# Linear attention's normaliser moved from the numerators to phi(Q), and the output weight folded into KV

## The chip, the cores and the metric

The kernel runs on one core of a Trainium2 chip. The metric is device time in microseconds for one execution. The engines named below are TensorE (PE, with its weight loads shown apart as PEld), VectorE (DVE), ScalarE (ACT), GpSimd (POOL) and SyncE (SP, which issues DMAs here).

## The reference, cut to what matters

Two attention branches read the same input x (2048 tokens, 512 features, 32 heads of 16) and are mixed by a gate per token:

```python
g = sigmoid((x * gate_w).sum(-1, keepdims=True))
# A: softmax attention
p = softmax(einsum("bhqd,bhkd->bhqk", q, k) * Dh**-0.5)
a = einsum("bhqk,bhkd->bhqd", p, v) -> (S, D) @ A_wo
# B: linear attention, own q, k, v from B_wqkv
phi = lambda t: where(t > 0, t + 1, exp(t)) + 1e-6
kv  = einsum("bhsd,bhse->bhde", phi(k), v)
z   = phi(k).sum over s
num = einsum("bhqd,bhde->bhqe", phi(q), kv)
den = einsum("bhqd,bhd->bhq", phi(q), z) + 1e-6
b   = (num / den) -> (S, D) @ B_wo
out = g * a + (1 - g) * b
```

Branch B can be regrouped: num @ B_wo equals, head by head, phi(q) @ (kv @ B_wo), and a division by den that is the same for all 16 columns of a head may be applied to phi(q) before either product.

## The kernel before, in words

**Scores.** A round is one query chunk of 512 tokens for four heads; there are 32 rounds. A round has 64 units, each a 128x512 tile of scores (one key block of 128, one head), 2048 units in all. A loop over groups (from L2160) takes two or three units at a time: TensorE computes their scores into PSUM banks 0 to 5, and one ScalarE instruction (L2239) takes the exp of all of them into the ring PT. Beside them VectorE "claims" further units: `claim` (near L1746) has TensorE write one more score tile into a spare bank or an unused third bank of a group, and VectorE turns it into an approximate exponential by writing integers that are read as float16 (DP). Four claimed units make a buffer; two shifted copies of it are made by an integer add, which GpSimd does nearly always (L1790) and VectorE otherwise (L1787). TensorE multiplies each PT tile by V once and each claimed tile by V three times (the copy and its two shifts, with weights), into an accumulator bank; at a round's end VectorE evicts it (L1475), and the softmax denominators travel by small DMAs on SyncE to a reciprocal and back, broadcast to `rbc`, for a product on VectorE (L1463).

**Everything else** (projections, branch B, the output) is a list of steps. A step runs TensorE pieces into the one spare bank (bank 7 and the accumulator's bank change places from time to time) and ends with VectorE or ScalarE work that empties it. While the bank is held by a step it can't carry a claimed unit. The steps have due times, spread over the groups: branch B's run from the 6th to about the 310th.

**Who sets the order.** The program is written out straight by a planner in Python that keeps a clock for every engine with estimated durations. It fills the time between two groups: products with V, a due step, a claim, in an order set by thresholds (class K, `OPTIONS`). The list `ORDER` picks a value for each threshold anew for every window of eight groups, so each row changes what follows. VectorE's waiting work is a pool of items (`push`), picked by priority and estimated start. A claim is taken only if the estimated VectorE backlog is below a threshold, a bank is free and a DP buffer is free. GpSimd and VectorE work without PSUM operands are kept from overlapping as far as the planner's estimates go: a GpSimd instruction waits for the last such VectorE instruction.

**Branch B before.** `step_BK` (16 steps): phi(K), by `phi_post`: an exp on ScalarE (L1136) and two VectorE instructions (L1139, L1141). `step_gate` and `step_Z`: rows of sums that VectorE copies to SBUF (L1126, L1196) and four small DMAs turn into columns (L1095). `step_M` (4): x times phi(K), evicted at L1175. `step_KV`: KV for all heads, masked to its diagonal blocks (L1215). `step_BQ` (16): phi(Q) of a chunk of 512 queries. `step_den` (4): 1/den times (1-g)/g for 512 tokens x 32 heads (L1242 to L1245). `step_num` (16, one per 128 tokens): phi(Q) times KV, evicted with a product by 1/den on VectorE (L1267) into `OB`, and a DMA transpose (L733) into `OBT`, the operand of the output matmuls. `step_out` (its first eviction starts at 518.7 us) accumulates branch B's and branch A's output in one bank and scales it by g on eviction (L1332).

Of the kernel before, what the change touches and what calls it, by code (L numbers as in the profile page):

```python
# [22 lines left out]
class K:  # L23
# [28 lines left out]
    ('EVEN', (2, 0, 5, 8)),  # L52
)
ORDER = [
    "000000000000000000000000",
    "000000000000000000000000",
    "000000000000000000000000",
    "000000000000000000000000",
    "000000000000000000000000",
    "000000000001000000000000",  # L60
    "000000200201000000000000",
    "000000000000000000000000",
    "000000000000000000000000",
    "000000200000000000100000",
    "000000000000000000000002",
    "000000000000000000000000",
    "000000000000000000000000",
    "000000000000000000002001",
    "010000001000000000000000",
    "000000200000000000000000",  # L70
    "000000000000000000000000",
    "000000000000000000000000",
    "000000000000000000000000",
    "000001000200000000000000",
    "000001000200020000000000",
    "000000200000000000000000",
    "000000000001000000000000",
    "000000030000000000000000",
    "000000030001000000000000",
    "000000000002000000000000",  # L80
    "100000200002000000000000",
    "000000000000000000000000",
    "000100200000000000100000",
    "000100200100000001100000",
    "000000030000000000000000",
    "000020030002001000000000",
    "000020000000000000000000",
    "000020000100000000000000",
    "000000000000000000000000",
    "000010000000001000000003",  # L90
    "200010000000001000000003",
    "000000000000000000000000",
    "000000000000000000000000",
    "000000100000000000000000",
    "000002020000000000000000",
    "000000000000000010000000",
    "000000000000020000000000",
    "000020000000020000020000",
    "000000000000000000000000",
    "000000000001000001000000",  # L100
    "000000000000000000000002",
    "000000000000000000000000",
    "000000000000000000000000",
    "000000002000200001000000",
    "010000202000200011002000",
    "000000000000020000001000",
    "000000000100200000000000",
    "200020000000000000100000",
    "200020200000100000200000",
    "200020200100100000001000",  # L110
    "000000010100000000000000",
    "000000000000000000000000",
    "000000000000000010000010",
    "000000000002000010000010",
    "000000000000000000000000",
    "000000000000000000000000",
    "000000000000000010000000",
    "000000100000000000000000",
    "010000100000000000200000",
    "000000000000000000020010",  # L120
    "000000000110000000000000",
    "200000000100010000000000",
    "000000200000010000000000",
    "000000002000000000000000",
    "000000012000000000000000",
    "000000000000000000000001",
    "010001000000000000000000",
    "000000000000000100000000",
    "000000000100000000000000",
    "300000000200000000000000",  # L130
    "000000000000000000000000",
    "000020200000010000000000",
    "200020200000010000200000",
    "000000000002000000000000",
    "000000000001010000000000",
# [27 lines left out]
E_MAX = 1.0e26  # L163
# [102 lines left out]
class _Res:  # L266

    __slots__ = ("name", "w", "r", "tw", "tr", "we", "pend", "pw")

    def __init__(self, name):  # L270
        self.name = name
        self.w = None
        self.r = {}
        self.tw = 0.0
        self.tr = 0.0
        self.we = None
        self.pend = 0
        self.pw = 0

# [58 lines left out]
def bass_gated_mix__mha_block__linear_attn_block__prompt_kernel(  # L338
# [33 lines left out]
    with ExitStack() as es:  # L372
# [66 lines left out]
        Zsel = SB([128, NCC, 8], BF16, "Zsel")  # L439

        phiK = SB([128, 2, 4, D], BF16, "phi")
        phiQT = phiK

        xnat = phiQT[:].rearrange("p a i n -> p (a i n)").rearrange("p (b c) -> p b c", b=NTB)
        rdB = SB([128, 2, 128], FP32, "rdB")

        OB = SB([128, 4, D], BF16, "OB")
        MT = OB
# [4 lines left out]

        def obt(tb):
            if tb < NTB // 2:
                return wB[:, :, D + 128 * tb:D + 128 * (tb + 1)]
            return OBT2[:, :, 128 * (tb - NTB // 2):128 * (tb + 1 - NTB // 2)]
# [6 lines left out]
        wide = OB[:].rearrange("p a n -> p (a n)").bitcast(FP32)[:, 0:512]  # L464
# [29 lines left out]
        semN = [SEM(f"s_n{k}") for k in range(5)]  # L494
        n_counts = [0] * 5
        semOB = [SEM(f"s_ob{b}") for b in range(NTB)]
# [9 lines left out]
        r_wA, r_warm, r_wB, r_woA, r_woB = R("wA"), R("warm"), R("wB"), R("woA"), R("woB")  # L506
# [8 lines left out]
        r_PT = [R(f"PT{i}") for i in range(NPT)]  # L515
        r_DP = [[R(f"DP{i}{k}") for k in range(NTRI)] for i in range(NB)]
# [15 lines left out]
        r_phiQT = r_phiK  # L532
        r_rdB = [R("rdB0"), R("rdB1")]
        r_OB = [R(f"OB{i}") for i in range(4)]
        r_OBT = [R(f"OBT{b}") for b in range(NTB)]
# [5 lines left out]
        r_wide = r_OB[0:2] + r_MT  # L541
# [49 lines left out]
        def blocker(it, reads, writes):  # L591
            for other in sorted((x for x in items if x.seq < it.seq), key=lambda x: x.seq):
                if any(conflicts(o, reads, writes) for o in other.ops):
                    return other
            return None
# [44 lines left out]
        def settle(reads, writes):  # L640

            while True:
# [82 lines left out]

        def flush_items():
            while items:
                it = min(items, key=lambda i: i.seq)
                emit_item_op(it)
# [40 lines left out]
        def dma_batch(pairs, sem, reads, writes, total_after, lands=3.0):  # L770
# [5 lines left out]
            SP.t = st + 0.59 * len(pairs)  # L776
# [78 lines left out]
        for t in range(1, NQC):  # L855
# [5 lines left out]
        op(PO, lambda: nc.gpsimd.memset(gw[:], 0.0), writes=[r_gw], dur=0.1)  # L861
        dma(gw[:, :, 0:1], gate_w.rearrange("(cc p o) -> p cc o", p=128, o=1), semG, writes=[r_gw], total_after=16, noncontig=True, E=SP,
            lands=8)
        xt_all = [r_xT[c][t] for c in range(NCC) for t in range(NQC)]
# [45 lines left out]
        op(PO, lambda: nc.gpsimd.memset(ones32[:, 0:1], 1.0), writes=[r_ones32], dur=0.1)  # L910
        op(PO, lambda: nc.gpsimd.memset(dev[:], OK_MID), writes=[r_dev], dur=0.2)
# [84 lines left out]
        def step_K(t8, t, early=False, on_act=False, lo=0, n=512, **kw):  # L996
# [4 lines left out]
            def post(b):  # L1001
                src = bank_ap(b)[:, 0:n]
                if on_act:
                    op(AC, lambda: nc.scalar.copy(KT[:, par, c0:c1], src), reads=[r_bank[b]],
                       writes=[r_KT[par][t]], dur=0.16 + n * 8.3e-4)
                    return
                push(1, [(lambda: nc.vector.tensor_copy(KT[:, par, c0:c1], src),  # L1007
                          [r_bank[b]], [r_KT[par][t]], d_psum(n), None)])
# [17 lines left out]
        def step_Q(t8, qc, early=False, **kw):  # L1026
# [3 lines left out]
            def post(b):  # L1030
# [8 lines left out]
                push(1, [(lambda: nc.vector.tensor_scalar(Qs[:, src, :], bank_ap(b), CQ, None, op0=ALU.mult),  # L1039
# [6 lines left out]
        def step_V(t8, v, early=False, **kw):  # L1046
# [13 lines left out]
            def post(b):  # L1060
# [14 lines left out]
                push(1, ops)  # L1075
# [13 lines left out]
        def row_to_columns(dst, sem, r_dst):  # L1089

            settle(r_wide, r_dst)
            st = est_start(SP, r_wide, r_dst)
            deps = _deps_for(r_wide, r_dst)
            for j in range(4):
                SP.add(lambda j=j: nc.sync.dma_start(dst(j), wide[32 * j:32 * j + 1, :]), deps, inc=False, dma_sem=sem, dma_val=64)  # L1095
            SP.t = st + 0.59 * 4
            for res in r_wide:
# [7 lines left out]

        def step_gate(**kw):
            rd = xt_all + [r_gw]

            def pieces(b):
                o = bank_ap(b)  # L1110
                fns = [[f_row(o, j, gw[:, cc, :], xT[:, cc, 512 * j:512 * (j + 1)], start=(cc == 0), stop=(cc == NCC - 1))
                        for j in range(4)] for cc in range(NCC)]
                return [(fns[k] + fns[k + 1], rd, 2 * MM512, 2 * MM512, "cols") for k in (0, 2)]

            def post(b):
                def moved():
                    row_to_columns(lambda j: eg[:, 4 * j:4 * j + 4], semRow[0], [r_eg])
                    push(1, [(lambda: nc.vector.tensor_single_scalar(eg[:], eg[:], -1.0, ALU.mult), [r_eg], [r_eg], 0.18, negated)])

                def negated():  # L1120
                    op(AC, lambda: nc.scalar.activation(eg[:], eg[:], ACT.Exp), reads=[r_eg], writes=[r_eg], dur=0.25, issue=0.2)  # L1121
                    push(1, [
                        (lambda: nc.vector.tensor_single_scalar(gom[:, 1, :], eg[:], E_MAX, ALU.min), [r_eg], [r_g], 0.18, None),
                        (lambda: nc.vector.tensor_single_scalar(gom[:, 0, :], gom[:, 1, :], 1.0, ALU.add), [r_g], [r_g], 0.18, None),
                        (lambda: nc.vector.reciprocal(gom[:, 0, :], gom[:, 0, :]), [r_g], [r_g], 0.25, None)])
                push(1, [(lambda: nc.vector.tensor_copy(wide.rearrange("p (q k) -> p q k", k=4), bank_ap(b).rearrange("p (k q) -> p q k", k=4)), [r_bank[b]], r_wide, d_psum(512) + 0.06, moved)])  # L1126
# [1404 lines left out]
```

## Time and profile before

| what | value |
|---|---|
| median of 3 runs | 656.63 us (656.48 to 656.77) |
| span of the profiled execution, first to last instruction | 655.0 us (the page gives no other time of it) |
| ScalarE busy | 641.3 us, 98% |
| TensorE busy / weight loads | 637.0 us, 97% / 188.3 us, 29% |
| VectorE busy | 577.0 us, 88% |
| GpSimd busy | 366.6 us, 56% |
| granted TensorE clock | 1.000 |

A row of a group of instructions reads: line, engine, operation, tile written and tile read, shapes, count, then total busy time, mean time of one in ns, and the idle time of the engine just ahead of them with what ended it. L826 is the line of a helper that records every matmul, so matmuls are told apart by their tiles. A row of a table by stretch gives the stretch, its length, the busy time of PE, PEld, DVE, ACT and POOL with counts, then the granted clock, the DMA engines' share and GB/s; limited to one line of the kernel, only its engine is given.

### The profile page before, as it was taken

How to read it: one execution, taken by the hardware profiler on the slowest of the kernel's cores; microseconds unless marked ns; L12 is line 12 of the kernel's file. 1: busy time of each engine (PE TensorE's matmuls, PEld its weight loads, DVE VectorE, ACT ScalarE, POOL GpSimd, SP SyncE). 2: the span in 40 equal slices, each digit the busy share in tenths (PEclk: the TensorE clock that was granted, in tenths of full speed). 3: DMA queues.
4: the chain of work that ended last, by engine and by line, in shares of the span. 5: the costliest groups of instructions: out<-in, count | busy, mean ns of one | idle time of the engine just before them, and what ended most of it. 6: DMA issues, size and time to landing. Idle time of an engine off the chain costs nothing.

```text
span 655.0 us, 18894 instructions
## 1 busy us (share of the span) xinstructions
PE 637.0 (97%) x7881; PEld 188.3 (29%) x7881; DVE 577.0 (88%) x994; ACT 641.3 (98%) x702; POOL 366.6 (56%) x365
## 2 busy tenths in 40 slices
PE   8999999999999999999999999999999999999997
PEld 4322222332223233233222233232222222222223
DVE  6588999989888887999999999999989989879984
ACT  5999999999999999999999999999999999999995
POOL 6055566555565554544474656566767656646650
PEclk9999999999999999999999999999999999999999
DMA  9900101001022010101202002020101001010111
GB/s 212 272 6 8 29 3 32 6 11 28 3 56 46 15 23 3 35 11 28 41 11 45 16 15 39 17 53 11 27 11 27 19 23 39 18 43 19 43 26 38
DMA packets 45968, 22.97 MB, mean 35 GB/s; under 512 B 35128, under 2 KB 41720, under 8 KB 45880
## 3 DMA queue, kind: packets, MB, share of 16 engines
q1 hardware_dynamic: 43864, 20.14, 13.9%
q10 hardware_dynamic: 2016, 1.57, 0.9%
q8 instruction: 65, 1.06, 0.7%
q14 instruction: 23, 0.19, 0.1%
HBM read 8.00 MB, written 2.10 MB: 15 GB/s over the span
## 4 chain that ended last, share of the span: by engine, by line
ACT 81%; PE 18%; DVE 0%; issue 0%; POOL 0%; ACTq 0%; POOLq 0%
ACT PT L2239 79%; PE ps L826 17%; ACT epool L1136 2%; PE ps L833 0%; DVE DP L2341 0%; DVE Qpad L1035 0%; DVE KT L1007 0%; DVE DP L2346 0%; DVE flag L2351 0%; POOL warm L871 0%; POOL gw L861 0%; POOL dummy L843 0%; ACT eg L1121 0%; ACTq L2454 0%; POOLq L2516 0%
## 5 line engine op out<-in xcount | busy, mean ns | idle before, releaser
L2239 ACT ACTIVATE PT<-ps 128x1024 bf16<-128x1024 f32 (+1 forms) x662 | 632.1, 1211 | 1.2 <-PE ps L826 0.9
L1790 POOL INT64_ADD DP<-DP x345 | 355.3, 1040 | 267.3 <-DVE DP L1746 201.1
L1746 DVE TENSOR_SCALAR DP<-ps 128x512 int16<-128x512 f32 x694 | 451.6, 683 | 42.4 <-PE ps L826 37.1
L826 PE MATMUL ps<-Qpad,KT 32*128 32x512 bf16 x2048 | 261.6, 384 | 11.3 <-ACT PT L2239 5.4
L826 PE MATMUL ps<-DP,Vaug 128*32 128x512 f16 x2077 | 200.2, 384 | 0.0
L826 PE MATMUL ps<-PT,Vaug 128*32 128x512 bf16 x1344 | 156.9, 384 | 1.0 <-DVE oraw L1475 0.5
L826 PEld LDWEIGHTS ps<-Qpad,KT 32*128 32x128 bf16 x2048 | 66.4, 91 | 282.9 <-ACT PT L2239 258.5
L826 PEld LDWEIGHTS ps<-DP,Vaug 128*32 128x32 bf16 x2077 | 47.1, 95 | 61.7 <-issue 42.8
L826 PEld LDWEIGHTS ps<-PT,Vaug 128*32 128x32 bf16 x1344 | 36.6, 94 | 44.2 <-issue 36.1
L826 PE MATMUL ps<-xT,wA 128*32 128x512 bf16 x432 | 33.0, 384 | 0.0
L1136 ACT ACTIVATE epool<-ps 128x512 bf16<-128x512 f32 x32 | 26.2, 817 | 0.0
L1475 DVE COPY oraw<-ps 128x512 f32<-128x512 f32 x31 | 21.1, 680 | 1.0 <-PE ps L826 1.0
L826 PE MATMUL ps<-warm 128*32 128x512 bf16 (+1 forms) x113 | 20.4, 401 | 1.2 <-POOL warm L871 1.2
L826 PE MATMUL ps<-wB,xT 128*32 128x512 bf16 x256 | 19.7, 384 | 0.0
L826 PE MATMUL ps<-xT,wB 128*32 128x512 bf16 x256 | 19.1, 384 | 0.0
L826 PE MATMUL ps<-woA,OT 128*32 128x512 bf16 (+1 forms) x226 | 18.9, 384 | 0.0
L1141 DVE SCALAR_TENSOR_TENSOR phi<-ps,epool 128x512 bf16<-128x512 f32 x24 | 16.5, 686 | 0.5
L1139 DVE TENSOR_SCALAR epool<-epool 128x512 bf16<-128x512 bf16 x32 | 9.3, 292 | 6.7 <-ACT epool L1136 6.3
L1007 DVE CAST KT<-ps 128x512 bf16<-128x512 f32 (+1 forms) x16 | 10.7, 666 | 5.2 <-PE ps L826 5.2
L826 PE MATMUL ps<-wA,xT 128*128 128x128 bf16 x192 | 14.9, 220 | 0.0
L1062 DVE CAST Vaug<-ps 128x512 bf16<-128x512 f32 x16 | 10.9, 682 | 2.3 <-PE ps L826 2.3
L826 PEld LDWEIGHTS ps<-wA,xT 128*128 128x128 bf16 x192 | 10.8, 98 | 5.4 <-issue 4.5
(115 smaller groups left out, 224.0 us busy)
## 6 DMA issues: line engine op xcount, KB each, us to landing
rbc<-oraw SPq DMA_DIRECT2D x16, 256.0 KB
OT<-in_A_x_dram SPq DMA_DIRECT2D x4, 512.0 KB, 7.3
Qpad<-Qs SPq DMA_DIRECT2D x124, 16.0 KB, 1.8
oraw<-oraw SPq DMA_DIRECT2D x60, 32.0 KB, 1.9
wA<-in_A_wqkv_dram SPq DMA_DIRECT2D x1, 1536.0 KB, 7.9
wB<-in_B_wqkv_dram SPq DMA_DIRECT2D x1, 1536.0 KB, 8.9
out_dram<-outt SPq DMA_DIRECT2D x12, 128.0 KB, 1.7
phi<-in_A_x_dram ACTq DMA_DIRECT2D x3, 256.0 KB, 6.0
```

Source lines behind the costliest of these rows:

```text
L826: return lambda: nc.tensor.matmul(o, lhsT=l, rhs=r, start=start, stop=stop, skip_group_check=sg)
L1007: push(1, [(lambda: nc.vector.tensor_copy(KT[:, par, c0:c1], src), [r_bank[b]], [r_KT[par][t]], d_psum(n), None)])
L1062: ops = [(lambda: nc.vector.tensor_copy(v_group(NQC * par + v)[:, :, :, 0:16], src), [r_bank[b]], [r_V[par][v]], d_psum(512), lambda: v_do ...
L1136: op(AC, lambda: nc.scalar.activation(epool[:, s, :], bank_ap(b), ACT.Exp), reads=[r_bank[b]], writes=[r_e[s]], dur=0.6, issue=0.48)
L1139: (lambda: nc.vector.tensor_scalar(epool[:, s, :], epool[:, s, :], 1.0, 1e-6, op0=ALU.min, op1=ALU.add), [r_e[s]], [r_e[s]], 0.29, None),
L1141: (lambda: nc.vector.scalar_tensor_tensor(out=dst, in0=bank_ap(b), scalar=0.0, in1=epool[:, s, :], op0=ALU.max, op1=ALU.add), [r_bank[b], ...
L1475: push(0, [(lambda: nc.vector.tensor_copy(oraw[:, half, :], acc), [r_acc], [r_oraw[half]], d_psum(512), evicted)])
L1746: push((0 if in_group else 1) + K.PRIO_NEW, [(lambda: nc.vector.tensor_scalar(DP[:, i, 512 * k:512 * (k + 1)].bitcast(I16), bank_ap(b), FR ...
L1790: ops = (*ops[:4], None, POOL_ADD, lambda z=z, i2=i2, i=i, n=n: nc.gpsimd.int64_add(DP[:, i2, 0:n].bitcast(I64), DP[:, i, 0:n].bitcast(I64 ...
L2239: op(AC, lambda p0=p0, b0=b0, n=n: nc.scalar.activation(PT[:, 512 * p0:512 * p0 + n], ps[:, 512 * b0:512 * b0 + n], ACT.Exp, scale=LN2 / F ...
```

## The change

- KV times the output weight: the KV step exchanges its operands, so that KVbd holds KV transposed, and four new steps (`step_W`) multiply it by each 128 rows of B_wo and write the result over `woB`. The numerators (`step_num`), their buffer OB and the 16 DMA transposes are gone.
- phi(Q) of each chunk is written straight to the place from which the output matmuls read it (`phiq`), and multiplied there by 1/den: `step_den` computes the denominators with heads along the partitions (Zsel has 32 columns now), VectorE adds, inverts and scales as before in three instructions, four DMAs gather the result into rows, four DMAs spread each head's row over its 16 partitions, and GpSimd makes four products of 128x512 per chunk (16 in all).
- The spreading DMAs are issued late: `later` holds them back until the planner's clock says that the gathered rows have landed.
- The gate step comes after KV. Its exp reads the bank directly on ScalarE, with the sign in its scale; VectorE's wide copy, its sign flip and one small step go. Its columns come in another order (`gcol`).
- The memset of gw becomes a GpSimd copy after its load; Zsel gets a memset.
- Five more thresholds can vary (`NEW_LATE`, `PRIO_EV`, `MARGIN`, `MIN_LAST`, `THIRD`), and `ORDER` is another list. The first option of each new threshold is the old constant, or no effect, except that `PRIO_EV` of 1 is the old priority of evictions and -1 puts them first.
- The planner counts thirds of units in whole numbers instead of fractions, and skips some searches.

```diff
+    ('NEW_LATE', (0, 1)),
+    ('PRIO_EV', (1, -1)),
+    ('MARGIN', (0.19, 0.1, 0.3)),
+    ('MIN_LAST', (20, 12, 28)),
+    ('THIRD', (30, 3)),
 )
 ORDER = [
...
+        later = []
+        def go_later(now=1e9):
+            while later and later[0][0] <= now:
+                later.pop(0)[1]()
...
-        op(PO, lambda: nc.gpsimd.memset(gw[:], 0.0), writes=[r_gw], dur=0.1)
+        push(1, [(lambda: nc.gpsimd.tensor_copy(gw[:, :, 1:32], gw[:, :, 0:1].to_broadcast([128, NCC, 31])), [r_gw], [r_gw], 0.0, None, 0.35)])
...
             def post(b):
-                def moved():
-                    row_to_columns(lambda j: eg[:, 4 * j:4 * j + 4], semRow[0], [r_eg])
-                    push(1, [(lambda: nc.vector.tensor_single_scalar(eg[:], eg[:], -1.0, ALU.mult), [r_eg], [r_eg], 0.18, negated)])
...
+                op(AC, lambda: nc.scalar.activation(gq.rearrange("p t q -> p q t"), bank_ap(b).rearrange("p (q t) -> p q t", q=NQC),
+                                                    ACT.Exp, scale=-1.0), reads=[r_bank[b]], writes=r_gqs, dur=0.6, issue=0.48)
+                row_to_columns(lambda j: eg[:, 4 * j:4 * j + 4], semRow[0], [r_eg], lambda j: gq[32 * j:32 * j + 1, :, :], r_gqs)
+                push(1, [
+                    (lambda: nc.vector.tensor_scalar(gom[:, 1, :], eg[:], E_MAX, 1.0, op0=ALU.min, op1=ALU.add), [r_eg], [r_g], 0.18, None),
+                    (lambda: nc.vector.reciprocal(gom[:, 0, :], gom[:, 1, :]), [r_g], [r_g], 0.25, None)])
...
+        def step_W(i, **kw):
+            rd = [r_KVbd, r_woB[i]]
+            def pieces(b):
+                return [(f_cols(bank_ap(b), KVbd[:, i, :], woB[:, i, :]), rd, MM512, MM512, "cols")]
+            def post(b):
+                push(K.PRIO_EV, [(lambda: nc.vector.tensor_copy(woB[:, i, :], bank_ap(b)), [r_bank[b]], [r_woB[i]], d_psum(512), None)])
+            return Step(pieces, post, reads=rd, **kw)
...
         def step_den(qc, **kw):
...
+                return [([f_mm(o[32 * m:32 * m + 32, 0:128], Zsel[:, i, :], phiq(qc)[:, i, 128 * m:128 * (m + 1)],
+                               start=(i == 0), stop=(i == NCC - 1), sg=True) for i in range(NCC) for m in range(4)],
+                         rd, 0.25, 0.1, "cols")]
...
+                def inverted():
+                    ndma(5, [(rows_[0:32, 128 * m:128 * (m + 1)], rdc[32 * m:32 * m + 32, :]) for m in range(4)], r_rdB[1:], r_wide)
+                    later.append((r_wide[0].tw + LAT, spread_out))
+                def spread_out():
+                    ndma(6, [(rdb[:, p, i, :], parts(rows_, 8 * i, [[1, 8]], [[0, 16], [1, 512]])) for i in range(NCC)],
+                         r_wide, r_rdb[p])
+                    for i in range(NCC):
+                        push(1, [(lambda i=i: nc.gpsimd.tensor_tensor(phiq(qc)[:, i, :], phiq(qc)[:, i, :], rdb[:, p, i, :], ALU.mult),
+                                  [r_rdb[p][i], r_PQ[qc][i]], [r_PQ[qc][i]], 0.0, None, POOL_TT)])
...
-        def step_num(tb, **kw):
...
-                push(1, [(lambda: nc.vector.tensor_tensor(dst, src, rv, ALU.mult), [r_bank[b], r_rdB[p]],
-                          [r_OB[s]] + (r_MT if tb < 4 else []),
-                          d_psum(512), after)])
...
-        b_steps += [step_gate(), step_Z()] + [step_M(c) for c in range(NCC)] + [step_KV()] + first_q
+        b_steps += [step_Z()] + [step_M(c) for c in range(NCC)] + [step_KV(), step_gate()]
+        b_steps += [step_W(i) for i in range(NCC)]
         for qc in range(NQC):
...
+            b_steps += [step_BQ(qc, i) for i in range(NCC)]
+            if qc:
+                b_steps.insert(len(b_steps) - 3, step_den(qc - 1))
+        b_steps.append(step_den(NQC - 1))
...
+            go_later(PE.t)
...
+                if (K.NEW_LATE and g > last_stage and hold[0] is None and not reserved() and bank_free(PE.t) is not None
+                        and due_step(PE.t)[0] is not None):
+                    first = int((t_late - PE.t - enter - NEW_T) / SET_T + K.ROOM)
+                    if first > 0 and pv_step(PE.t, most=min(first, K.MOST)):
+                        continue
```

392 lines of the change are left out of this document (190 added, 202 removed).

## The prediction

> **What bounds the kernel now.** I read the page's busy times and its chain first, then the groups with their shapes kept apart, then busy times by stretch, then the waits.
>
> ```profile
> span 655.0 us, 18894 instructions
> PE 637.0 (97%) x7881; PEld 188.3 (29%) x7881; DVE 577.0 (88%) x994; ACT 641.3 (98%) x702; POOL 366.6 (56%) x365
> ACT 81%; PE 18%; DVE 0%; issue 0%; POOL 0%; ACTq 0%; POOLq 0%
> ...
> L2239 ACT ACTIVATE PT<-ps 128x1024 bf16<-128x1024 f32 x630 | 592.6, 1195 | 0.3 <-PE ps L826 0.2
> L1746 DVE TENSOR_SCALAR DP<-ps 128x512 int16<-128x512 f32 x694 | 451.6, 683 | 42.4 <-PE ps L826 37.1
> L1790 POOL INT64_ADD DP<-DP x345 | 355.3, 1040 | 267.3 <-DVE DP L1746 201.1 <-DVE epool L1139 22.1 <-DVE OT L1463 11.1
> L826 PE MATMUL ps<-DP,Vaug 128*32 128x512 f16 x2077 | 200.2, 384 | 0.0
> L2239 ACT ACTIVATE PT<-ps 128x1536 bf16<-128x1536 f32 x31 | 45.0, 1542 | 0.9 <-PE ps L826 0.7
> ```
>
> The score work is 2048 tiles ("units") of 128x512. ScalarE takes 630x2 + 31x3 and one alone, 1354; VectorE claims the other 694 (L1746), whose copies GpSimd makes (L1790). ScalarE idles about 1.2 us ahead of all its score groups together. So nothing shortens this kernel except fewer instructions on ScalarE: another claimed unit, or a cheaper other step there. The Trainium skill (Perfetto Trace Analysis, Identifying the Most-Contended Engine) warns that matmul busy time is no measure of TensorE's headroom; the trace agrees in so far as a TensorE 97% busy leaves ScalarE practically never waiting.
>
> The price of a unit comes from the chain of waits, start to start:
>
> ```profile
> 400.87 0.49 ACT epool L1136
> 401.36 106.77 ACT PT L2239 x116
> ```
>
> 106.77/116 = 0.920 us for a group of two, 0.460 us a unit. (The 1195 ns of the group's row overlap their neighbours.)
>
> What keeps VectorE from claiming more is read by stretch; the first table is all engines (PE, PEld, DVE, ACT, POOL), the second is L1746 alone:
>
> ```profile
> 40.00:160.00 120.00, 117.49 (x1472) 34.26 (x1473) 109.90 (x187) 120.00 (x139) 67.04 (x65) 1.00 0.08 16
> 160.00:280.00 120.00, 118.67 (x1538) 34.71 (x1534) 104.04 (x176) 120.00 (x131) 66.95 (x65) 1.00 0.12 25
> 280.00:460.00 180.00, 176.21 (x2140) 52.97 (x2132) 171.23 (x298) 180.00 (x203) 103.67 (x101) 1.00 0.13 26
> 460.00:520.00 60.00, 57.72 (x668) 14.70 (x667) 56.45 (x95) 60.00 (x67) 41.49 (x41) 1.00 0.10 20
> 520.00:600.00 80.00, 79.87 (x1014) 21.02 (x1010) 69.33 (x111) 79.81 (x86) 47.34 (x46) 1.00 0.12 31
> ...
> 280.00:460.00 180.00, 131.32 (x204) 1.00 0.13 26
> 460.00:520.00 60.00, 51.04 (x82) 1.00 0.10 20
> ```
>
> From 280 to 460 us, where the numerators stand, VectorE is busy 171.23 of 180 us (95%) and claims 1.13 units a us; from 460 to 520, with none of that work, the same share gives 82/60 = 1.37. There VectorE's time is what limits the claims. From 520 to 600 it is 87% busy and the limit is another one (a free bank, TensorE).
>
> **The change, part by part.** What VectorE and ScalarE do today in the linear branch and the gate:
>
> ```profile
> L1267 DVE TENSOR_TENSOR OB<-ps,rdB 128x512 bf16<-128x512 f32 x16 | 10.9, 680 | 0.2 <-PE ps L826 0.2
> L1175 DVE CAST OB<-ps 128x512 bf16<-128x512 f32 x4 | 2.7, 680 | 0.0
> L1126 DVE COPY OB<-ps 128x512 f32<-128x512 f32 x1 | 0.7, 680 | 0.0
> L1124 DVE TENSOR_SCALAR gom<-gom 128x16 f32<-128x16 f32 x1 | 0.2, 175 | 0.0
> L1118 DVE TENSOR_SCALAR eg<-eg 128x16 f32<-128x16 f32 x1 | 0.2, 165 | 0.0
> L1195 DVE TENSOR_TENSOR Zsel<-zc,maskK 128x32 bf16<-128x32 f32 x1 | 0.2, 191 | 0.0
> L1121 ACT ACTIVATE eg<-eg 128x16 f32<-128x16 f32 x1 | 0.4, 370 | 0.0
> ```
>
> *VectorE.* Sixteen numerator evictions go: 16 x 0.680 = 10.88. The gate loses its wide copy (0.680), its sign flip (0.165) and one of three small steps (0.175). In all 11.90 us. Four evictions of KV times weight come, like L1175: 4 x 0.680 = 2.72; Zsel is written by four small steps for one, about 3 x 0.18 = 0.53. The three steps of a denominator stay three, of the same sizes. Net freed: 11.90 - 3.25 = 8.65 us, nearly all of it between 280 and 460 us, where VectorE limits. At 683 ns a claim that is 12.7 units. The other requirement of a claim, a bank, agrees: 16 steps that held the spare bank go and 4 come, 12 openings.
>
> *ScalarE.* The gate's exp now reads 128x512 from a bank, like the epool step of the chain (0.49), for the 0.370 of L1121, which may overlap its neighbours. Added: 0.1 to 0.5; I take 0.3.
>
> *GpSimd.* Sixteen products phi(Q) x 1/den, 128x512 bf16 with two SBUF inputs, are not in this trace. Nearest rows: the same width with two inputs on VectorE is 0.680 (L1463 below), the INT64_ADD is 1.040 for 512 items from one input, twice that is 2.08. I take 1.3, the add and a quarter, since the product reads one more input: 16 x 1.3 = 20.8 us (10.9 to 33.3). Between 280 and 460 us GpSimd has 180 - 103.67 = 76.3 us free, and 11 further units want 5.5 more adds (5.7 us). It is hidden at either end. If that cover were gone, copies of claimed units would come late, their buffers free late, and claims stop: each add not made in time holds back two units, 0.92 us of ScalarE.
>
> *The port between them.* GpSimd waits for VectorE instructions whose operands all lie in SBUF. The waits and two rows:
>
> ```profile
> POOL DP L1790 <- DVE DP L1746: 201.1, 143, 17.5
> POOL DP L1790 <- DVE epool L1139: 22.1, 19, 2.1
> POOL DP L1790 <- DVE OT L1463: 11.1, 9, 1.9
> ...
> L1139 DVE TENSOR_SCALAR epool<-epool x32: 281/294/297, 32.1 to 401.4; 128x512 bf16<-128x512 bf16 x32
> L1463 DVE TENSOR_TENSOR OT<-oraw,rbc x15: 677/680/682, 81.2 to 626.0; 128x512 bf16<-128x512 f32 x15
> ```
>
> The program makes GpSimd wait for such VectorE work (22.1 and 11.1 us), and that work shows no stretching: 281 to 297 ns over 32 instances. So the cost falls on GpSimd, which mostly waits for claims anyway (201.1). Bounds for VectorE's loss: nothing, or all 20.8 us of products. I take 1 us, 1.5 units, near the lower end since 104 us of adds already lie in that stretch and VectorE reaches 95% beside them. The Trainium skill (SBUF — State Buffer, Who interferes with whom) speaks against the change here: the shared port pair is an exclusive lock, held for a whole instruction, and a two-input VectorE instruction from SBUF contends with a GpSimd one that reads SBUF. By that rule at its worst, every product blocking VectorE from start to end, the sum would come out slower; that is the second rival.
>
> *TensorE.*
>
> ```profile
> L826 PE MATMUL ps<-KVbd,phi 128*128 128x128 bf16 x64 | 6.4, 222 | 0.0
> L826 PE MATMUL ps<-Zsel,phi 128*128 128x8 bf16 x64 | 2.2, 167 | 0.0
> L826 PE MATMUL ps<-woB,wB 128*32 128x512 bf16 x128 | 9.7, 384 | 0.0
> ```
>
> Out go the numerators' 6.4 us and the old denominators' 2.2, and the turns between full and column-tiled matmuls. In come 16 column-tiled ones for the weights (at 9.7/128 = 0.076: 1.2 us) and 64 of 128 columns for the denominators, between 2.2 us (today's) and 64 x 0.076 = 4.9. Net -5.2 to -2.5. Each extra unit has three products for one: 2 x 200.2/2077 = 0.193, so 11 units take 2.1 back. TensorE breaks even or gains; I count nothing. If TensorE instead fed ScalarE late, each us would count whole.
>
> *SyncE and DMA.*
>
> ```profile
> L733 SPq DMA_TRANSPOSE wB<-OB x8: 1204/1282/2095, 292.2 to 352.5; - x8
> L1095 SPq DMA_DIRECT2D eg<-OB x4: 566/602/602, 159.5 to 161.4; - x4
> L775 SPq DMA_DIRECT2D rbc<-oraw x16: 610/636/642, 73.5 to 635.0; - x16
> SPq L733 <- DVE OB L1267: 9.4, 2, 7.3
> L1332 DVE TENSOR_SCALAR outt<-ps,gom x12: 740/743/750, 518.7 to 624.7; 128x512 bf16<-128x512 f32 x12
> ```
>
> Sixteen transposes go, some 16 x 1.28 = 20.5 us of issue, which stood in the queue ahead of Qpad fills and softmax broadcasts and waited there for L1267. For each of four query chunks come four gathers (0.602 like eg's) and four spreads: 0.636 like the softmax broadcast, or up to a transpose's 2.1. That is 20 to 43 us of issue over the 160 us of those steps. The spread waits for the gather's landing; because it is issued late, the fills behind it do not queue behind that wait. Only output blocks read the result, first evicted at 518.7, some 70 us after the last numerator of today. Cost nothing. Without that cover the spreads would delay a Qpad fill, and a round could not start.
>
> *Five thresholds and a new list.* They decide every stretch anew, so their effect has both signs. Best: VectorE's 94% of 460 to 520 also in 160 to 280 and 520 to 600, (0.94 x 200) - 104.04 - 69.33 = 14.6 us, 21 units, -9.8 us. Worst: the 87% of those stretches also in 280 to 460, 171.2 - 156 = 15 us, +10.2. Nothing in the profile leans either way: zero.
>
> **Sum.** 12.7 - 1.5 = 11.2 units x 0.460 = 5.15, less 0.3 for the gate: 4.85 us. The profiled span is 655.0 and becomes 650.2. The page gives no other time of that execution; the median of the runs, 656.63, is 1.63 above the span, which I keep: 651.8. Converting 60% of the freed time, or a few units more by the thresholds, makes this 649 to 655.
>
> **The rivals.** *One: the relief is not converted.* VectorE simply idles more, because banks or TensorE decide the claims. For it: 520 to 600, where VectorE idles 10.7 us of 80 with TensorE busy 79.87. Against: the numerators stand where VectorE is at 95%. Time: 656.63 + 0.3 = 656.9.
>
> *Two, slower: the products stall VectorE.* Place: 280 to 460 us. Each product holds what VectorE's SBUF-only work needs (reciprocal, epool, OT), and every claim queued behind that waits. It eats the gain from 8.65/16 = 0.54 us a product on. At 0.8: 12.8 - 8.65 = 4.15 us, 6.1 units, 2.8 + 0.3 = 3.1 us: 659.7. Full 1.3: 12.15 us, 17.8 units, 665.1. Against it stands L1139's even 281 to 297.
>
> *Three: the thresholds add as well.* Half of their best, 4.9 us, on top: 646.9. For it: the 13% of VectorE idle in two stretches; against: TensorE at 99% there.
>
> **How the numbers follow.** Forecast 0.60; one 0.14; two 0.13; three 0.13. This kernel's measurement tells 0.2%, 1.3 us, from no change. Faster: 0.59 of the forecast, 0.13 of three and 0.04 of one, 0.76. Same: 0.01 and 0.09 of one, 0.10. Slower: two and 0.01 of one, 0.14. The range holds the forecast (649 to 655 by itself) and reaches a little past the points of one and three, 646.4 to 657.2, which takes in some 0.2 of their 0.27.
>
> **What would show it.** L1746's count near 705 and ScalarE's pairs near 624: right. VectorE's share from 280 to 460 still about 95%: converted; at 90% with the same count: rival one. SBUF-only VectorE rows longer than now, or new waits on GpSimd: rival two. Claims up outside 280 to 460: rival three. Products above 4 us each, or ScalarE idle in mid-span, would prove me wrong in a way that I have not priced.

## The result, and the profile after

The changed kernel takes 701.67 us (median of 5 runs, 700.56 to 704.8) beside 656.48 us of the kernel before on the same chip: a ratio of 1.0695, interval 1.0677 to 1.0712. It is 45 us slower, where 4.85 us were forecast to be gained. The profiled execution took 701.88 us, its span is 700.0.

The page of the changed kernel: busy times, ScalarE's and the clock's rows in 40 slices, and the chain by engine.

```profile
span 700.0 us, 18910 instructions
PE 639.1 (91%) x7881; PEld 185.5 (27%) x7881; DVE 579.2 (83%) x997; ACT 637.1 (91%) x690; POOL 389.9 (56%) x387
ACT  6999999999999999999999993948976929999996
PEclk9999999999999999999999996978987969999999
...
ACT 55%; PE 30%; issue 6%; POOL 4%; DVE 3%; DMA 1%; POOLq 0%; ACTq 0%
```

ScalarE does less work than before (637.1 us for 641.3) in a longer span. Its row has four deep holes, from the 25th slice on (a slice is 17.5 us), and the granted clock falls in the same slices. The chain, 81% ScalarE before, now has 6% "issue", which is time in which an engine waited for nothing that the profile shows, and 4% GpSimd.

The groups of the changed kernel, shapes kept apart:

```profile
L2265 ACT ACTIVATE PT<-ps 128x1024 bf16<-128x1024 f32 x610 | 577.0, 1185 | 49.4 <-PE ps L855 49.1
L1776 DVE TENSOR_SCALAR DP<-ps 128x512 int16<-128x512 f32 x708 | 457.9, 685 | 87.6 <-PE ps L855 83.7
L2265 ACT ACTIVATE PT<-ps 128x1536 bf16<-128x1536 f32 x40 | 58.0, 1511 | 1.4 <-PE ps L855 1.2
L1290 POOL TENSOR_TENSOR wB<-wB,phi 128x512 bf16<-128x512 bf16 x8 | 9.4, 1198 | 14.0 <-issue 7.1 <-DVE DP L1776 6.9
L1290 POOL TENSOR_TENSOR OBT<-OBT,phi 128x512 bf16<-128x512 bf16 x8 | 9.0, 1148 | 14.2 <-issue 7.2 <-DVE DP L1776 7.0
```

VectorE claims 708 units for 694: in sum, the relief was converted. But ScalarE idles 49.4 + 1.4 = 50.8 us ahead of its score groups, where it idled 1.2 before, and TensorE ends that idle time. The last two rows are the sixteen products on GpSimd: 1.15 to 1.20 us each, and 28.2 us of idle time in front of them, of which half is put down to nothing ("issue").

The first of four visits of the products to GpSimd, in the timeline. Columns: start, length, engine, work, and in brackets the idle time ahead with what ended it.

```profile
414.71 1.04 POOL L1820 INT64_ADD DP<-DP  x1 [1.72 <-DVE rdB L1297]
422.68 4.47 POOL L1290 TENSOR_TENSOR wB<-wB,phi 128x512 bf16<-128x512 bf16 x4 [6.94 <-DVE DP L1776]
433.30 5.09 POOL L1820 INT64_ADD DP<-DP  x5 [6.15 <-issue]
...
434.38 0.62 PE L855 MATMUL ps<-DP,Vaug 128*32 128x512 f16 x4 [11.05 <-POOL DP L1820]
...
415.39 9.32 ACT L2265 ACTIVATE PT<-ps 128x1024 bf16<-128x1024 f32 x10
436.44 1.02 ACT L2265 ACTIVATE PT<-ps 128x1024 bf16<-128x1024 f32 x1 [11.74 <-PE ps L855]
```

GpSimd ends an add at 415.75, does nothing for 6.94 us, makes four products in 4.47 us, does nothing for 6.15 us, and adds again at 433.30: 17.55 us without a copy. TensorE runs its instructions in the order in which the program lists them, and none of the later ones starts in this gap; its next one in line multiplies a claimed copy, and it stands 11.05 us for it. ScalarE, fed by TensorE, stands 11.74 us. The release by L1776 (DVE) in the second row does not explain the length of that wait: two of the four visits show the same gap (7.06 and 7.18 us) with "issue", which names no other engine.

The waits of the changed kernel (in total, times, longest, us):

```profile
ACT PT L2265 <- PE ps L855: 50.3, 15, 12.3
PE ps L855 <- POOL DP L1820: 44.0, 5, 12.0
POOL DP L1820 <- issue: 24.1, 4, 6.1
```

Read from below: four returns to the add cost 24.1 us, 6.0 each; TensorE waits 44.0 us for late copies, ScalarE 50.3 us for TensorE.

Busy times by stretch of the changed kernel (stretch, length, PE, PEld, DVE, ACT, POOL, then the granted clock):

```profile
420.00:424.00 4.00, 3.30 (x39) 0.78 (x35) 3.73 (x7) 4.00 (x6) 1.32 (x2) 1.00 0.35 71
424.00:428.00 4.00, 0.00 (x0) 0.00 (x0) 0.38 (x1) 0.71 (x1) 3.15 (x3) 0.64 0.10 23
428.00:432.00 4.00, 0.00 (x0) 0.00 (x0) 0.00 (x0) 0.00 (x0) 0.00 (x0) 0.50 0.25 36
436.00:440.00 4.00, 4.00 (x37) 1.23 (x34) 2.96 (x5) 3.03 (x4) 2.38 (x3) 0.65 0.14 26
440.00:444.00 4.00, 3.88 (x52) 1.35 (x49) 4.00 (x9) 4.00 (x5) 2.21 (x3) 1.00 0.01 2
```

From 428 to 432 nothing computes at all. TensorE's clock drops to 0.50 while it stands and is back at 1.00 in the stretch from 440, so it restarts slowly: 37 matmuls in 4 us for 52. Read in stretches of 0.5 and 1 us over the four stalls, the clock falls 1.8 to 2.2 us after the end of the last matmul and is full again 3.5 to 5.7 us after the restart. The Trainium skill (TensorE: Matmul & The Clock Gate, Part 1) says that the clock halves after an idle window of about 3.4 us and recovers after as long a busy one. This trace agrees on the halving; the fall came sooner here, and the recovery took as long or longer.

One kind of row tells the two kernels apart. Instructions of the add's and the product's line, changed kernel (duration, first and last start), and then of the add's line before:

```profile
L1290 POOLq MODIFY_POOL_CONFIG  x8: 11/11/11, 415.7 to 553.0; - x8
L1820 POOLq MODIFY_POOL_CONFIG  x10: 1/6/11, 21.0 to 564.8; - x10
```

```profile
L1790 POOLq MODIFY_POOL_CONFIG  x2: 11/11/11, 15.5 to 15.6; - x2
```

Two instructions of 1 to 11 ns in GpSimd's sequencer stand at each change between the add and the product: 8 for four changes to it, 8 more for four changes back, beside the 2 at the start. The first of them starts at 415.7 us, where the add before it ends, so the gap lies behind them. The Trainium skill (GPSIMD Engine Reference, Instruction dispatch) says that the first call to freshly loaded GpSimd code pays about 6 us for its loading, which no instruction of the profile shows. This trace agrees on the size, 5.79 to 6.15 us back to the add and about a microsecond more, 6.94 to 7.18, into the product; and it shows the price at every change, not only the first. That the gap is a loading of code is not shown here: the instruction queue of the DMA table moves 1.06 MB with the changes and without them. What the runs below show is a price at each change of kind; "change of code" is short for that.

### The profile page after: what moved, and what is told of

It reads as the page before. It is cut to its first block, busy times and chain, and to the rows that moved or that the text cites. A ratio compares the mean times of both kernels' runs of the same rounds, so it can differ in the third digit from the quotient of the medians.

```text
span 700.0 us, 18910 instructions
## 1 busy us (share of the span) xinstructions
PE 639.1 (91%) x7881; PEld 185.5 (27%) x7881; DVE 579.2 (83%) x997; ACT 637.1 (91%) x690; POOL 389.9 (56%) x387
## 3 DMA queue, kind: packets, MB, share of 16 engines
q8 instruction: 65, 1.06, 0.7%
## 4 chain that ended last, share of the span: by engine, by line
ACT 55%; PE 30%; issue 6%; POOL 4%; DVE 3%; DMA 1%; POOLq 0%; ACTq 0%
ACT PT L2265 54%; PE ps L855 30%; DVE DP L1776 2%; POOL DP L1820 1%; ACT epool L1166 1%; POOL wB L1290 1%; POOL OBT L1290 1%; DMA PT<-in_A_x_dram 1%; DVE DP L2372 0%; DVE oraw L1506 0%; DVE KT L1037 0%; ACT MT L1151 0%; PE ps L862 0%; DVE Qpad L1065 0%; DVE xT L2099 0%
## 5 line engine op out<-in xcount | busy, mean ns | idle before, releaser
L2265 ACT ACTIVATE PT<-ps 128x1024 bf16<-128x1024 f32 (+1 forms) x650 | 627.1, 1205 | 50.8 <-PE ps L855 50.3
L1776 DVE TENSOR_SCALAR DP<-ps 128x512 int16<-128x512 f32 x708 | 457.9, 685 | 87.6 <-PE ps L855 83.7
L1820 POOL INT64_ADD DP<-DP x350 | 359.9, 1038 | 256.8 <-DVE DP L1776 151.7
L855 PE MATMUL ps<-DP,Vaug 128*32 128x512 f16 x2118 | 204.9, 392 | 34.2 <-POOL DP L1820 33.9
L1290 POOL TENSOR_TENSOR wB<-wB,phi 128x512 bf16<-128x512 bf16 x8 | 9.4, 1198 | 14.0 <-issue 7.1
L1290 POOL TENSOR_TENSOR OBT<-OBT,phi 128x512 bf16<-128x512 bf16 x8 | 9.0, 1148 | 14.2 <-issue 7.2
L1169 DVE TENSOR_SCALAR epool<-epool 128x512 bf16<-128x512 bf16 x32 | 10.5, 329 | 3.3 <-ACT epool L1166 2.8
L1092 DVE CAST Vaug<-ps 128x512 bf16<-128x512 f32 x16 | 10.9, 683 | 2.3 <-PE ps L855 2.3
```

Of the source, the lines that this page charges most:

```text
L855: return lambda: nc.tensor.matmul(o, lhsT=l, rhs=r, start=start, stop=stop, skip_group_check=sg)
L1092: ops = [(lambda: nc.vector.tensor_copy(v_group(NQC * par + v)[:, :, :, 0:16], src), [r_bank[b]], [r_V[par][v]], d_psum(512), lambda: v_do ...
L1169: (lambda: nc.vector.tensor_scalar(epool[:, s, :], epool[:, s, :], 1.0, 1e-6, op0=ALU.min, op1=ALU.add), [r_e[s]], [r_e[s]], 0.29, None),
L1290: push(1, [(lambda i=i: nc.gpsimd.tensor_tensor(phiq(qc)[:, i, :], phiq(qc)[:, i, :], rdb[:, p, i, :], ALU.mult), [r_rdb[p][i], r_PQ[qc][i ...
L1776: push((0 if in_group else 1) + K.PRIO_NEW, [(lambda: nc.vector.tensor_scalar(DP[:, i, 512 * k:512 * (k + 1)].bitcast(I16), bank_ap(b), FR ...
L1820: ops = (*ops[:4], None, POOL_ADD, lambda z=z, i2=i2, i=i, n=n: nc.gpsimd.int64_add(DP[:, i2, 0:n].bitcast(I64), DP[:, i, 0:n].bitcast(I64 ...
```

## The experiments

Theory S: changing GpSimd between the add and the product costs some 13 us a visit, in which no copies are made. Its rivals: D, the products wait for late spreading DMAs; P, the products' own run time and the shared port; L, the new list of thresholds is bad. For D little spoke before any run: the spreads for the second chunk were issued from 428.79 to 434.5 us, and the products that read them began at 458.62, with the same 7.06 us of "issue" ahead.

### The same program without the change of code

```diff
- nc.gpsimd.tensor_tensor(phiq(qc)[:, i, :], phiq(qc)[:, i, :], rdb[:, p, i, :], ALU.mult)
+ nc.gpsimd.int64_add(phiq(qc)[:, i, :].bitcast(I64), phiq(qc)[:, i, :].bitcast(I64), 0)
```

> Each of the 16 products on GpSimd is replaced by an integer add of zero to the same tile (so phi(Q) is left without its factor 1/den), with the same waits; the order of instructions on all other engines is the same as in the changed kernel. Theory S (GpSimd loads other code whenever it changes between the integer add and the product, some 7 us there and 6 us back, four times): the stalls are gone, 650 to 654 us, granted clock 1.00. Rival D (the spreading DMAs land late and hold GpSimd's queue): the stand-ins wait for the same DMAs, 690 to 702 us. Rival P (a product holds the port that VectorE needs): the stand-ins are shorter, but the stalls stay in kind, above 680 us.

Measured: 651.35 us, ratio 0.9918, interval 0.9902 to 0.9935. Its page, groups and timeline:

```profile
PE 631.9 (97%) x7879; PEld 185.4 (29%) x7881; DVE 576.5 (89%) x997; ACT 635.7 (98%) x690; POOL 378.3 (58%) x387
```

```profile
L2265 ACT ACTIVATE PT<-ps 128x1024 bf16<-128x1024 f32 x610 | 576.6, 1206 | 0.9 <-PE ps L855 0.8
L2265 ACT ACTIVATE PT<-ps 128x1536 bf16<-128x1536 f32 x40 | 58.5, 1523 | 0.9 <-PE ps L855 0.7
L1776 DVE TENSOR_SCALAR DP<-ps 128x512 int16<-128x512 f32 x708 | 457.6, 685 | 39.8 <-PE ps L855 35.8
```

```profile
416.58 1.53 POOL L1290 INT64_ADD wB<-wB  x4 [0.84 <-DVE epool L1169]
418.08 2.06 POOL L1820 INT64_ADD DP<-DP  x2
```

Same DMAs, same waits, same list, same order on the other engines: the holes are gone. Against this run the changed kernel's span is 700.0 - 649.5 = 50.5 us longer; ScalarE's idle time ahead of score groups is 50.8 - 1.8 = 49.0 of it, its busy time 637.1 - 635.7 = 1.4. That closes the account. D and L fall, since both are unchanged here. Of P, the run time alone is 16 x (1.17 - 0.38) = 13 us of GpSimd, not 50, and the port shows as no more than the 579.2 - 576.5 = 2.7 us by which VectorE is busier in the changed kernel.

### The products on VectorE

```diff
- nc.gpsimd.tensor_tensor(phiq(qc)[:, i, :], phiq(qc)[:, i, :], rdb[:, p, i, :], ALU.mult)   # POOL_TT
+ nc.vector.tensor_tensor(phiq(qc)[:, i, :], phiq(qc)[:, i, :], rdb[:, p, i, :], ALU.mult)    # d_sb(512, 0.5)
```

> The 16 products run on VectorE, 0.42 to 0.69 us each, 6.7 to 11 us of its time. Theory S: no change of code on GpSimd, no stall; VectorE gives back most of what it gained: 654 to 658 us. Rival D: VectorE stands at the head of its own queue for late spreads, above 670 us. Rival P: as S, 654 to 658 us.

Measured: 662.54 us, ratio 1.0090, interval 1.0074 to 1.0107, above the expectation. Its page and a group:

```profile
PE 638.6 (97%) x7900; PEld 187.8 (28%) x7901; DVE 573.6 (87%) x997; ACT 642.7 (97%) x695; POOL 363.3 (55%) x362
L1290 DVE TENSOR_TENSOR OBT<-OBT,phi 128x512 bf16<-128x512 bf16 x8 | 3.0, 419 | 0.0
```

No stall is left, and the whole computation is done: 39 us come back. What it misses of the run before is 17 claims (691 for 708), when sixteen products of 0.42 us, 6.7 us, would pay for ten. VectorE is less busy than there (573.6 for 576.5 us), so its time alone does not explain the rest. A list that no longer fits may; the last two sections of experiments take that up.

### Fewer visits

The products of two chunks are handed to GpSimd together.

```diff
+ held_q.append(products)
+ if qc % 2:
+     while held_q:
+         held_q.pop(0)()
```

> The products of two chunks are handed to GpSimd together: two batches of eight instead of four of four. Theory S: two of the four stalls go (50 us of ScalarE's idle time in four, 12.5 each) and the other two grow by up to the 4.5 us of four more products: 674 to 687 us. Rivals D and P: the number of products and spreads is the same, 695 to 705 us.

Measured: 691.16 us, ratio 1.0528, interval 1.0511 to 1.0546. The timeline of GpSimd shows three visits, not the two that I had counted on (the planner put adds between the first two chunks), and its pairs of units in the groups:

```profile
437.96 4.52 POOL L1293 TENSOR_TENSOR wB<-wB,phi 128x512 bf16<-128x512 bf16 x4 [7.46 <-DMA phi<-MT]
458.65 4.53 POOL L1293 TENSOR_TENSOR wB<-wB,phi 128x512 bf16<-128x512 bf16 x4 [7.19 <-issue]
534.82 10.31 POOL L1293 TENSOR_TENSOR OBT<-OBT,phi 128x512 bf16<-128x512 bf16 x8 [6.91 <-DVE DP L1824]
```

```profile
L2272 ACT ACTIVATE PT<-ps 128x1024 bf16<-128x1024 f32 x605 | 574.4, 1189 | 29.4 <-PE ps L855 29.2
```

The same sixteen products with one visit less: ScalarE's idle time falls from 49.4 to 29.4 us. Three times some 7 us stands in front, with three different releasers beside it. The number missed the expectation (674 to 687) by that third visit and by 20 claims lost (688 for 708). The 20 us less of idle time are more than the 12.5 that one visit was to give, so this run does not by itself part "a price a visit" from "where the visits lie"; the next run does.

### One product in the kernel before

One of the products of the softmax normalisation (L1463, 15 in the trace) is moved from VectorE to GpSimd. Nothing of the change is in this kernel.

```diff
- on_pool = OT_POOL and r < NR - 8
+ on_pool = r == 15
```

> The kernel before, with one single VectorE product (that of the softmax normalisation of round 15, 128x512) moved to GpSimd; no spreading DMA, no other change but the planner's order behind it. Theory S: one stall, 12.5 us less the 3.4 us of the three products that are not there: 662 to 669 us. Rival D: nothing of it here, 655 to 658 us. Rival P: at most that one product, 655 to 658 us.

Measured: 675.13 us, ratio 1.0282, interval 1.0265 to 1.0299. The chain of waits around it, and the row of that product:

```profile
363.94 7.41 issue
371.35 1.26 POOL OT L1463
...
378.45 1.04 POOL DP L1790
```

```profile
L2239 ACT ACTIVATE PT<-ps 128x1024 bf16<-128x1024 f32 x626 | 590.8, 1183 | 13.0 <-PE ps L826 12.8
L1463 POOL TENSOR_TENSOR OT<-oraw,rbc 128x512 bf16<-128x512 f32 x1 | 1.3, 1252 | 7.4 <-issue 7.4
```

A single product of 1.26 us opens a gap of 7.41 us ahead and 5.84 us behind (378.45 - 372.61), and ScalarE idles 13.0 us for 0.3. That is the price of a visit, without any other part of the change. (The trace puts the 5.84 us down to a claim that ended 0.14 us before the add; only their size, and the same gap with "issue" in the other runs, speak for the change.) The time went up by more than expected (662 to 669): ScalarE is also busy 4.5 us longer (645.8), probably since the planner's order was made for another program; that was not tested apart.

### The planner told of the price

The changed kernel, with 6.5 us added to the planner's clock of GpSimd at each change between add and product, in both directions.

```diff
+ kind = "tt" if other[0] == POOL_TT else "add" if len(other) > 1 else None
+ if kind is not None:
+     if kind != pool_kind[0] and pool_kind[0] is not None:
+         PO.t += SWITCH_POOL          # 6.5
+     pool_kind[0] = kind
```

> The changed kernel, with one thing added to the planner's clock: GpSimd's time moves on by 6.5 us whenever it changes between integer adds and products. The instructions are of the same kinds and the products are all there. If the loss is TensorE being sent to wait for copies that the planner believes done: ScalarE's idle time falls from 50 us to under 10, some claims are lost while GpSimd is away, 657 to 672 us. Rival (GpSimd's absence itself starves the kernel, whatever the order): 685 to 702 us.

Measured: 660.7 us, ratio 1.0060, interval 1.0043 to 1.0076. Groups:

```profile
L2272 ACT ACTIVATE PT<-ps 128x1024 bf16<-128x1024 f32 x602 | 569.3, 1210 | 0.7 <-PE ps L862 0.7
L1824 DVE TENSOR_SCALAR DP<-DP 128x2048 int16<-128x2048 int16 x31 | 21.5, 712 | 0.0
L1297 POOL TENSOR_TENSOR OBT<-OBT,phi 128x512 bf16<-128x512 bf16 x8 | 9.1, 1154 | 17.4 <-issue 7.2 <-DVE DP L1783 7.0 <-DVE DP L1824 1.3
```

There are still four visits with their gaps (third row), and ScalarE waits for none of them: an order that knows of them gives the copies of those stretches to VectorE, 31 at 0.71 us for the 4 of the run without the change of code, 26 of them between 420 and 530 us, where the visits lie. It pays for this with claims (685). So 41 us come back (701.67 - 660.7) from an order that knows the price, with the same products on the same engine.

### How much the list of thresholds is worth

First, the run without the change of code, and the planner told 0.5 us for each product instead of 1.3. Then that run, and the kernel before, each with no list at all, so that every threshold keeps its first value.

```diff
- [r_rdb[p][i], r_PQ[qc][i]], [r_PQ[qc][i]], 0.0, None, POOL_TT)])
+ [r_rdb[p][i], r_PQ[qc][i]], [r_PQ[qc][i]], 0.0, None, 0.5)])
```

> The integer stand-in for the products once more (phi(Q) without 1/den), but the planner is told 0.5 us for each instead of 1.3; nothing else. Theory L (the list of thresholds fits one exact plan, and any shift in it spoils what follows; that is why the products on VectorE cost 11 us where their own time explains 4.5): 656 to 668 us, fewer claims than 708. Rival (the list is robust): 650 to 653 us.

> The integer stand-in for the products (phi(Q) without 1/den) with an empty list, so that every window takes the first value of each threshold. Theory L: 665 to 675 us. Against the kernel before with an empty list it shows the gain of the regrouping alone: my term of 4.85 us says 3 to 7 us faster than that; if the gain of the stand-in came from the new list, no difference (within 2 us).

> The kernel before with an empty list. Theory L: 668 to 680 us, 3 to 7 us above the stand-in with an empty list. If lists are worth little: 655 to 660 us.

Measured: 662.22 us (ratio 1.0088, 1.0071 to 1.0105) with the other duration, with 696 claims for 708; 667.9 us (1.0170, 1.0153 to 1.0187) without the list; 672.88 us (1.0248, 1.0231 to 1.0265) for the kernel before without its list. The pages of the two without a list, the regrouped one first:

```profile
PE 645.5 (97%) x7902; PEld 184.7 (28%) x7904; DVE 562.2 (84%) x962; ACT 653.6 (98%) x708; POOL 350.7 (53%) x360
```

```profile
PE 653.1 (97%) x7952; PEld 192.6 (29%) x7954; DVE 561.5 (84%) x961; ACT 656.7 (98%) x712; POOL 343.7 (51%) x343
```

Three things follow. Sixteen estimated durations of an engine off the critical path, made 0.8 us shorter, cost 662.22 - 651.35 = 10.9 us, although 0.5 us is nearer to the 0.38 that the adds took: a list fits one exact plan. A list is worth 672.88 - 656.67 = 16.2 us to the kernel before and 667.9 - 651.35 = 16.6 us to the regrouped one, so the new list is no better than the old one was for its own program. And the regrouping by itself, without lists and without the change of code, gains 672.88 - 667.9 = 5.0 us, of which ScalarE's busy time is 656.7 - 653.6 = 3.1; the two intervals do not meet. Both figures of the regrouped program are those of stand-ins of 0.38 us in place of products of 1.15, so they bound what the regrouping can gain with the products on GpSimd.

### The products on VectorE, with another list

```diff
  ORDER: 33 rows, from the 49th on, replaced by values that a search on the planner's own clock found
```

> The sixteen products on VectorE, as in the run that measured 662.54, and from the 49th row of the list of thresholds on other values, searched so that the planner's own clock ends earlier for this program; the work is the same. Theory L (the list of the changed kernel fits one exact plan, and 662.54 was mostly its misfit): the claims go from 691 back towards 700, ScalarE's busy time falls from 642.7 to about 638 to 640, and the time to 656 to 660. Rival V (the products on VectorE are the cost: 16 x 0.417 = 6.7 us of an engine that limits the claims): the claims stay near 691 whatever the list, and the time at 661 to 664. By the net of VectorE's work, 8.65 us freed less 6.7 spent = 2 us, 3 units, 1.3 us, no list should bring it under 653.

Measured: 659.16 us, ratio 1.0042, interval 1.0026 to 1.0059. Its page:

```profile
PE 636.9 (97%) x7863; PEld 186.2 (28%) x7864; DVE 571.7 (87%) x994; ACT 642.4 (98%) x695; POOL 367.4 (56%) x366
```

The time is as theory L had it, the claims (692) as its rival had them. ScalarE's work is what it was (642.4 for 642.7). Its span is 657.0 for 660.8 us; of these 3.8, ScalarE's wait for TensorE ahead of two of the last outputs (L2366) makes 7.5 - 4.8 = 2.7, and its waits ahead of score groups 2.3 - 1.4 = 0.9. It stays open how far a better list would carry this version; no version that computes everything was found to beat the kernel before.

## Why the prediction was wrong, step by step

**The step that failed** is GpSimd's: "16 x 1.3 = 20.8 us (10.9 to 33.3) ... It is hidden at either end." The price of the instruction was right: 1.14 to 1.20 us, and the sixteen take 18.4 us. What was missing is what lies between a product and an add: in the trace four times some 7 us before and some 6 us after, 52 us that are no instruction, on top of the 18.4. I compared the sum with 76.3 us free in a stretch of 180. Each visit is one block of 17.55 us, though, and the cover has to be there in that block: the free time of GpSimd comes in waits of 1.4 us on the mean (201.1/143 for L1746). The planner had the same blind spot: it was told 1.3 us a product and nothing for the change, so it sent TensorE to wait for copies that it believed done. Told of the gaps, it found cover for them, at 660.7 us.

**The price for the cover gone** came near, by another path. The forecast said that "claims stop: each add not made in time holds back two units, 0.92 us of ScalarE". At GpSimd's 58% (103.67/180) a block of 17.55 us holds 9.8 adds, 9.0 us. Measured: 49.0/4 = 12.3 us a visit. But the claims did not fall, they rose to 708, and ScalarE had no more work to do (637.1 us for 641.3). It stood: TensorE, in the order of the program, waited for the late copies and made no score tiles for ScalarE either, and then restarted on a halved clock. That 9.0 lies near 12.3 is luck.

**"ScalarE idle in mid-span"** was written as what would prove me wrong in a way not priced, and it is what the trace shows. "Products above 4 us each" was the wrong thing to look for: the price stands beside the instruction, as idle time with a false releaser or none.

**VectorE and ScalarE: near in size, in part by luck.** ScalarE's busy time fell by 641.3 - 637.1 = 4.2 us for 4.85 forecast; claims rose by 14 for 11.2. Without the change of code the gain was 656.85 - 651.35 = 5.5 us with lists, 5.0 without. One term was small: the gate's exp took 1.17 us by its record, at most 0.8 more than L1121, for 0.1 to 0.5. Since the claims were not gained where the forecast had them (next point), the near sum does not show its mechanism.

**Their place: wrong.** "Nearly all of it between 280 and 460 us." VectorE's claims alone by stretch, run without the change of code, then the kernel before:

```profile
40.00:160.00 120.00, 93.65 (x147) 1.00 0.08 16
160.00:280.00 120.00, 97.65 (x153) 1.00 0.10 20
280.00:460.00 180.00, 125.33 (x193) 1.00 0.12 24
```

```profile
40.00:160.00 120.00, 85.74 (x131) 1.00 0.08 16
160.00:280.00 120.00, 86.36 (x131) 1.00 0.12 25
```

And all engines in the run without the change of code (PE, PEld, DVE, ACT, POOL):

```profile
160.00:280.00 120.00, 117.02 (x1442) 32.88 (x1439) 113.38 (x195) 120.00 (x132) 77.95 (x76) 1.00 0.10 20
280.00:460.00 180.00, 177.22 (x2267) 52.40 (x2264) 160.72 (x278) 179.56 (x199) 101.25 (x104) 1.00 0.12 24
```

Between 40 and 280 us there are 38 claims more, and between 280 and 460 there are 11 fewer (193 for 204). By my own list of signs that is rival three's ("claims up outside 280 to 460"), though the sum is the forecast's: VectorE's share rises from 87% to 94% between 160 and 280 us (113.38 of 120), and falls from 95% to 89% between 280 and 460 (160.72 of 180), where its time was to be the limit. The list is not all of it. In the two kernels without a list the regrouped one has 13 claims more between 40 and 280 us (254 for 241) and one fewer between 280 and 460 (187 for 188). One reason stands in the program: the planner spreads branch B's steps evenly over the same groups, and there are 47 now for 59, so fewer of them fall early. Between 40 and 160 us VectorE has 9 of phi's first steps (L1169) for 14 (L1139). No run moved the steps alone, so how much of the shift is theirs stays open.

**The port: small, as forecast, but larger.** Forecast 1 us of loss on VectorE, from rows that show no stretching. The row of epool in the changed kernel and in the run without the products:

```profile
L1169 DVE TENSOR_SCALAR epool<-epool 128x512 bf16<-128x512 bf16 x32 | 10.5, 329 | 3.3 <-ACT epool L1166 2.8
```

```profile
L1169 DVE TENSOR_SCALAR epool<-epool 128x512 bf16<-128x512 bf16 x32 | 9.3, 290 | 3.3 <-ACT epool L1166 2.8
```

1.2 us in this row; one instance took 1.236 us for a median of 0.294. The four adds left on VectorE (L1817) take 853 ns for 684, 0.7 us more in all, and VectorE's busy time as a whole differs by 2.7 us. Rival two, the stall through the port, put the slowdown at the right instructions and gave it the wrong cause: it would have cost VectorE's time, and these 2.7 us are all that VectorE lost by longer work.

**TensorE: right side.** Without the code change it is busy 631.9 us for 637.0, with 14 more claims in it, and ScalarE waits 1.8 us for it. **SyncE and DMA: right.** The run without the change of code keeps every DMA and loses nothing to them. **Five thresholds and a new list, "zero": right between two fitted lists** (16.6 against 16.2 us), but the bounds of 10 us on either side were narrow: one misfit cost 10.9 us, and no list at all 16. I had not seen that the list also ties the program to its estimated durations, so that any experiment on it pays some of this.

**Rivals one and three** did not decide the time: the claims rose in sum, and no further gain came on top. Each shows in a stretch, though: rival three's between 160 and 280 us, and rival one's, a VectorE that idles more, between 280 and 460.

## What to carry to other kernels

Before an engine is given an instruction of a kind that it has not had beside its present work, look for what separates the kinds, not only for what one costs: here a visit, two changes of kind on GpSimd, cost 13 us beside products of 1.15 us, and one single product cost the kernel 18 us, 12.7 of them in ScalarE's waits. Cover is a matter of the longest block, not of the sum: compare the block in which an engine is away with the time for which its consumers have work in hand. And tell the planner: with the price known to it, the same program lost 4 us instead of 45.

## What the runs showed of the hardware

The price between GpSimd's two kinds of work, the 64-bit add and the product, was not expected: 6.9 to 7.5 us into the product, 5.8 to 6.15 us back to the add, the same in the changed kernel, in the one with fewer visits, in the one whose planner knows of it and in the kernel before with one product, whether four, eight or one product stand between. It is paid again at each visit. The trace marks it only by two instructions of 1 to 13 ns in GpSimd's sequencer and by idle time whose releaser is "issue", or whichever event came last. What GpSimd does in that time the trace does not show, and which other pairs of instructions pay nothing was not tried.
